# A 7x7 convolution of a 224x224 image on one core: the last tile's stage C loads spread over rounds, its inverse matrices built a tile earlier, a longer filler

## The chip, the cores and the metric

The kernel runs on one core of a Trainium2 chip. The metric is the device time of one execution in microseconds (us). Five engines take part: TensorE (PE in the profile, with PEld for its weight loads), VectorE (DVE), ScalarE (ACT), GpSimd (POOL) and SyncE (SP), which here only issues DMAs. Transfers run on 16 DMA engines.

## The reference, cut to what matters

```python
H = W = 224; C = 96; K = 7            # x: (1, H, W, C) bf16, w: (K, K, C, C) bf16
wp = jnp.pad(w, ((0, H - K), (0, W - K), (0, 0), (0, 0)))
Xf = rfft2(x.astype(f32), axes=(1, 2))
Wf = rfft2(wp.astype(f32), axes=(0, 1))
Yf = jnp.einsum('bhwi,hwio->bhwo', Xf, Wf)
y  = irfft2(Yf, s=(H, W), axes=(1, 2)).astype(bf16)
```

This is a circular convolution of the image with a 7x7 filter, with 96 channels in and 96 out. The output has the shape of the image.

## The kernel before, in words

The kernel does not use large Fourier transforms. Along the rows of the image (h) it works on 8 blocks of B = 28 rows, each lengthened by 6 rows to L = 34, and transforms these by a small real Fourier transform of 17 frequencies (NS = 17, numbered s). Along the columns (w) it convolves directly with the 7 taps, in a form that shares products between even and odd pixels. The columns are cut into NT = 7 tiles of 32 pixels; a tile is t, the last one is TL = 6.

There are three stages, and at any time they run for different tiles:

- Stage A (a_jobs, a_mm) loads rows of the image into xn and transforms them by matmuls with the matrix Fm; the results go to xf in SBUF.
- Stage B (b_round, one call for each frequency s) does the convolution for one frequency. It computes sums and differences J of xf on DVE (jit, called for three frequencies at a time), does 33 to 34 small matmuls with the transformed weights WF, and combines the two PSUM banks by an ACT operation (tt_), two DVE operations (u and v) and a last sum into yf, on POOL or, where DVE makes it, on DVE. put_y stores yf to a DRAM tile after every third frequency: scr for the earlier tiles, and for the last tile scra (frequencies 0 to 8) and three tiles scrb (9 to 11, 12 to 14, 15 and 16).
- Stage C (c_jobs, c_bank) turns the frequencies back into rows. For every tile but the last, load_t reads scr back in six groups (two halves h of the tile's columns, three groups gi of row blocks) into the buffers tt. A group takes 2 to 4 DMAs, 15 in all. Matmuls with the matrix G follow, evictions into yo, and DMAs of yo to the output (put_o). The last tile is done in another way, at the end of the program: scra is read into tl_a (two DMAs) and the scrb tiles into tl_b (load_b, three DMAs), and each of 16 PSUM banks gets a matmul of tl_a with the matrix GA (function first) and one of tl_b with a matrix GB (function second).

The order of work is written out by hand. The loop `for t in range(2, NT)` (line 792) runs stage B of tile t in rounds s = 0 to 16, with stage A of tile t + 1 and stage C of tile t - 1 filled in between by pace: a list of jobs, with first and last slot, where slots are counted as 2s and 2s + 1 and the fills of a round come after its first and after its second half. In the last tile one job of tile 4 and five of tile 5 are done in the rounds; the other five of tile 5 (half h = 1) stay for the end (`while cj`, line 838). Every engine runs its instructions in the order of the program, and this includes SP's DMA issues. The pools are: 8 PSUM banks, 6 buffers tt, 4 buffers yo, 4 buffers yf.

The parts that the change and the prediction touch:

- pump (line 676) issues the pending stage C loads while fewer than NTT = 6 groups are held; queue_c (line 681), called in round 3 of a tile, puts the six groups of tile t - 1 into the list and calls it. The end of each group's job also calls it (line 663). The variable late is always 0.
- g_parts (line 617) is a generator that builds GB and GA out of G. Its first 24 steps write GB, in tiles 3 and 4. The next one sets GA to zero on POOL and copies a first part; each further step copies one more by a DMA of SP. GA has four parts. It lies in the memory of Fm (line 783), which stage A of the last tile reads until round 12 of tile 5; the profile therefore calls it Fm.
- In tile 6, load_b(0) is issued in round SL[2] + 2 = 14, and the two DMAs into tl_a in round SA + 1 = 10. tl_a and tl_b lie in the memory of xf.
- From frequency 9 on, the last tile's puts are held in the list puts and issued by ACT (put(SE)): one after ACT's operation of round 12, the next at the end of round 16. The put of frequencies 15 and 16 is SP's.
- After the rounds, load_b(1) and load_b(2) are issued, the rest of stage C runs, then eight matmuls first, then WARM = 16 filler matmuls (line 857). The filler adds zeros to the eighth bank; it has no part in the result. Then come the 16 matmuls second with their evictions, by DVE and ACT in turn (tail_evac), the other eight first among them.

```python
    def queue_c(t):
        pend.extend((t, i % 3, i // 3) for i in range(6))
        pump()
```

Of the kernel before, what the change touches and what calls it, by code (L numbers as in the profile page):

```python
# [16 lines left out]
NS = L // 2  # L17
# [21 lines left out]
CQ = {2: (10, 2), 3: (8, 4), 4: (6, 7), 5: (3, 9), 6: (1, 5)}  # L39
NXN = 2  # L40
NP2 = 0
WARM = 16


def slot(s, part):
# [4 lines left out]
def kernel(  # L50
# [10 lines left out]
    TL = NT - 1  # L61
# [92 lines left out]
    SA = SL[1]  # L154
# [280 lines left out]
    def a_jobs(t):  # L435
        xf = new_xf(t)
        jobs = []
        for jg in range(2):
            if t == 0:
                jobs.extend(a_bank(t, xf, xh_bufs[jg], 0, 3, jg, 0))  # L440
            c = 2 * t + jg
            for h in range(2):
                for (q, n) in ((0, 3), (3, 3), (6, 2)):
                    jobs.extend(a_bank(t, xf, xn_bufs[c % NXN], h * PXC + 2 * q, n, jg, HALO + h * 8 + q))
            last = jobs.pop()

            def fin(last=last, c=c):
                last()
                if c + NXN < NCH:
                    load_x(c + NXN)  # L450
            jobs.append(fin)
        return jobs
# [4 lines left out]
    def jit(t, g):  # L457
        s0, s1 = JGB[g]
        n = s1 - s0
        xf = xf_tiles[t][0:C]  # L460
        xv = xf.rearrange("c p r s w j -> c p r s (w j)")
        b = jcount[0] % 3 if t < 2 else (jcount[0] - 2 * len(JGB)) % 2
        jcount[0] += 1
        Jb = J_bufs[b][0:C].rearrange("c (k s q) -> c k s q", k=7, s=3)
        for s in range(s0, s1):
            jbuf[(t, s)] = Jb[:, :, s - s0]

        def sub(o, i0, i1, op, cost):
            def f():
                load["v"] += 170 + cost * n / 1.92  # L470
                return VE.tensor_tensor(out=o, in0=i0, in1=i1, op=op)
            return f
        x0, x1 = xv[:, 0, :, s0:s1], xv[:, 1, :, s0:s1]
        pd, rd, sd, qd = x1.ap
        dpl = bass.AP(x1.tensor, x1.offset - NJ, [pd, [NJ, 2], rd, sd, qd])
        return [
            sub(Jb[:, 0:4, 0:n].rearrange("c (k r) s q -> c k r s q", r=2), dpl,
                x0.unsqueeze(1).to_broadcast([C, 2, 2, n, PP]), ALU.subtract, 4 * PP),
            sub(Jb[:, 4, 0:n], xv[:, 0, 0, s0:s1], xv[:, 0, 1, s0:s1], ALU.add, PP),
            sub(Jb[:, 5:7, 0:n], Jb[:, 0:4:2, 0:n], Jb[:, 1:4:2, 0:n], ALU.add, 2 * PP),  # L480
        ]
# [110 lines left out]
    def load_t(t, gi, h):  # L592
        j0, nj = CG[gi]
        n = nj * FR
        tt = t_pool.tile([128, TW // 2, 2 * C], BF16, name="tt")
        tt_tiles[(t, gi, h)] = tt
        sv = scr_tiles[t].rearrange("w j s (r e) -> (j s r) w e", r=2)
        n0 = n // 16 * 16
        w0, w1 = (h * 8, (h + 1) * 8) if gi < 2 else (h * 6, (h + 1) * 6)
        for (p0, p1) in ((0, n0), (n0, n)):  # L600
            dma(tt[p0:p1, 0:w1 - w0], sv[j0 * FR + p0:j0 * FR + p1, w0:w1])
        if gi == 2:
            for j, wa, wb, q0 in REST[h]:
                dma(tt[n:n + FR, q0:q0 + wb - wa], sv[j * FR:(j + 1) * FR, wa:wb])
# [6 lines left out]
    def load_b(i, eng, nh):  # L611
        sb = scr_tiles[(TL, 1 + i)].rearrange("w j s (r e) -> (j s r) w e", r=2)
        for h in range(nh):
            w0, w1 = h * TW // nh, (h + 1) * TW // nh
            dorder(eng.dma_start(out=tl_b[KO[i]:KO[i] + KB[i], w0:w1], in_=sb[:, w0:w1]))
# [12 lines left out]
    def c_bank(tt, yo, k, nj):  # L628
        pb = bank()
        TE.matmul(pb[0:nj * B, 0:4 * C], lhsT=G[0:nj * FR, 0:nj * B],  # L630
                  rhs=tt[0:nj * FR, 2 * k:2 * k + 2, :].rearrange("p w e -> p (w e)"), start=True, stop=True)
        evac(yo[0:nj * B, k * 4 * C:(k + 1) * 4 * C], pb[0:nj * B, 0:4 * C], 4 * C)

    def put_o(t, yo, p0, j, nj, wa, wb, q0):
        px = t * 2 * TW + 2 * wa
        dma(out[0, j * B:(j + nj) * B, px:px + 2 * (wb - wa), :].rearrange("h w c -> h (w c)"),
            yo[p0:p0 + nj * B, q0 * 2 * C:(q0 + wb - wa) * 2 * C])

    def c_jobs(t):
        jobs = []  # L640
        for h in range(2):
            for gi in range(3):
                j0, nj = CG[gi]
                hold = {}

                def mk_(ks, done, h=h, gi=gi, j0=j0, nj=nj, hold=hold):
                    def f():
                        if ks[0] == 0:
                            hold["yo"] = yo_pool.tile([4 * B, PXC * C], BF16, name="yo")
                        tt = tt_tiles[(t, gi, h)]  # L650
                        yo = hold["yo"]
                        for k in ks:
                            c_bank(tt, yo, k, 3 if gi < 2 or h == 0 or k == 0 else 2)
                        if not done:
                            return
                        if gi < 2:
                            put_o(t, yo, 0, j0, nj, 8 * h, 8 * h + 8, 0)
                        else:
                            put_o(t, yo, 0, j0, nj, 6 * h, 6 * h + 6, 0)
                            for j, wa, wb, q0 in REST[h]:  # L660
                                put_o(t, yo, nj * B, j, 1, wa, wb, q0)
                        held[0] -= 1
                        pump()
                    return f
                if gi < 2:
                    jobs.extend((mk_((0, 1), False), mk_((2, 3), True)))
                else:
                    jobs.append(mk_((0, 1, 2), True))
        return jobs

    NTT = 6
    held = [0]
    late = [0]
    pend = []

    def pump():
        while len(pend) > late[0] and held[0] < NTT:
            load_t(*pend.pop(0))
            held[0] += 1

    def queue_c(t):
        pend.extend((t, i % 3, i // 3) for i in range(6))
        pump()

    def warm(n):
        p = bank()
# [51 lines left out]
    def add(a, b, jobs):  # L738
        qs.append([a, b, jobs, len(jobs)])
# [19 lines left out]
    for r in range(NS + LAG):  # L759
# [4 lines left out]
        for t in range(2):  # L764
            s = r - LAG * t
# [25 lines left out]
    gp = g_parts()  # L791
    for t in range(2, NT):
        if t == TL:
            scr_tiles[t] = None
            scr_tiles[(t, 0)] = dr_pool.tile([TW, NJ, SA, 4 * C], BF16, name="scra")
            for i in range(len(KB)):
                scr_tiles[(t, 1 + i)] = dr_pool.tile([TW, NJ, KB[i] // (2 * NJ), 4 * C], BF16, name=f"scrb{i}")
        else:
            scr_tiles[t] = dr_pool.tile([TW, NJ, NS, 4 * C], BF16, name="scr")
        qs = []  # L800
        if t + 1 < NT:
            add(0, 26, a_jobs(t + 1))
        nold, nnew = CQ[t]
        k1 = 2 * NS if t < TL else 2 * NS - 9
        k0 = 12 if t == 2 else 3
        km = max(13, k0 + -(-(k1 - k0) * nold // (nold + nnew)))
        add(k0, km, cj[:nold])
        cn = c_jobs(t - 1)
        cj = cn[nnew:]
        add(km, k1, cn[:nnew])  # L810
        plan = {}
        for g, (s0, s1) in enumerate(JGB):
            if g + 1 < len(JGB) or t + 1 < NT:
                plan[s0 if g + 1 < len(JGB) else s0 - 1] = g
        for s in range(NS):
            now = ()
            if s in plan:
                g = plan[s]
                now = jit(t, g + 1) if g + 1 < len(JGB) else jit(t + 1, 0)
            if s == 3:  # L820
                queue_c(t - 1)
            if t in (3, 4) and s < 12 or t == TL and s < 4:
                next(gp, None)
            if t == TL and s == SL[2] + 2:
                load_b(0, DE, 1)
            if t == TL and s == 0:
                late[0] = 0
            if t == TL and s == SA + 1:
                sv = scr_tiles[(TL, 0)].rearrange("w j s (r e) -> (j s r) w e", r=2)
                for g in range(2):  # L830
                    dma(tl_a[g], sv[g * KA:(g + 1) * KA])
                late[0] = 0
                pump()
            b_round(t, s, fills(qs, 2 * s), fills(qs, 2 * s + 1), bool(now) if t < TL else s >= NS - 2 or (s < 12 and bool(now)), now)
    tail[0] = 2
    load_b(1, DE, 1)
# [19 lines left out]
    live = {k: first(*k) for k in order[:8]}  # L856
    for _ in range(WARM):
        TE.matmul(live[order[7]].rearrange("p (a b) -> p a b", a=12), lhsT=Fm.rearrange("p r s j -> p (r s j)")[:, 0:M4],
# [48 lines left out]
```

## Time and profile before

| | |
|---|---|
| median of 4 runs | 281.85 us (283.61, 284.4, 280.08, 280.1) |
| the profiled execution | 283.61 us, span 281.9 us |
| mean granted TensorE clock | 0.959 |
| busy, share of the span | PE 93%, PEld 85%, DVE 84%, ACT 66%, POOL 35% |
| chain that ended last | PE 66%, DVE 15%, DMA 8%, ACT 5% |
| tile 6 from about 235 us to the last round's end | 23.75 us (235.00 to 258.75) |
| from there to the first matmul of tl_b with GB | 13.61 us |
| from there to the end | 9.54 us |

The span runs from the first to the last instruction; the rest of the execution's time lies around it. A busy share is an average over stages with different limits, so a stage is read from its own window and from the waits that end last in it. In the timeline, times are us from the span's start; a row gives start, length, engine, line, operation and the names out<-in, and in brackets how long the engine was idle before it and what ended that. All operations are recorded with the line of one helper (L82), so they are told apart by the names. SPq and ACTq are rows of an engine's DMA issues.

### The profile page before, as it was taken

To read this page: it belongs to the slowest core of one execution; us is meant where nothing else is said; L and a number is where in the kernel's file an instruction comes from. 1 tells how busy PE (TensorE), PEld (TensorE's weight loads), DVE (VectorE), ACT (ScalarE), POOL (GpSimd) and SP (SyncE) were. 2 spreads that over 40 slices of the span, in tenths; PEclk is the share of its full clock that TensorE was granted. 3 is DMA by queue.
4 is the path that set the end of the run, shared out by engine and by line. 5 is a ranking of instruction groups with operands and counts; after the bars stand their busy time and mean duration, and the time that the engine had idled before them with its cause. 6 is when DMAs were issued, how large, how long until landed. Compare 5 with 4: busy or idle time off the path is not lost.

```text
span 281.9 us, 11544 instructions
## 1 busy us (share of the span) xinstructions
PE 262.9 (93%) x4810; PEld 239.8 (85%) x4810; DVE 237.6 (84%) x500; ACT 185.4 (66%) x459; POOL 99.1 (35%) x134
## 2 busy tenths in 40 slices
PE   8599999999979999999999999999999999799692
PEld 3299899999979999998989998899989998698371
DVE  6269999999997799999878899878988899989323
ACT  5079887665613986987888768887788854462222
POOL 2741023266455433422422242233243225345000
PEclk9959999999979999999999999999999999999668
DMA  8686243111211468988775875794868542867765
GB/s 164 110 227 163 63 131 109 44 44 45 86 45 44 155 188 181 274 251 238 229 194 142 262 216 186 171 274 146 255 168 201 192 160 69 192 177 170 203 179 183
DMA packets 45284, 46.01 MB, mean 163 GB/s; under 512 B 33746, under 2 KB 35974, under 8 KB 45136
## 3 DMA queue, kind: packets, MB, share of 16 engines
q1 hardware_dynamic: 44816, 43.78, 55.9%
q10 hardware_dynamic: 416, 1.49, 2.3%
q8 instruction: 38, 0.62, 1.0%
q14 instruction: 14, 0.11, 0.2%
HBM read 23.92 MB, written 21.33 MB: 161 GB/s over the span
## 4 chain that ended last, share of the span: by engine, by line
PE 66%; DVE 15%; DMA 8%; ACT 5%; SPq 2%; issue 2%; DVEq 0%; POOL 0%; ACTq 0%
PE pb L82 66%; DVE J L82 5%; DMA wq<-in_w_dram 4%; ACT xf L82 3%; DVE v L82 3%; DVE WF L82 3%; DMA out_dram<-yo 2%; DVE u L82 2%; ACT WF L82 2%; SPq L82 2%; DMA tt<-scr 1%; DVE xf L82 1%; DVE yf L82 1%; DVE tt L82 0%; DMA xn<-in_x_dram 0%
## 5 line engine op out<-in xcount | busy, mean ns | idle before, releaser
L82 PE MATMUL pb<-WF,J 96*128 96x96 bf16 x2898 | 166.8, 207 | 1.8 <-DVE J L82 0.6
L82 PEld LDWEIGHTS <-J 96*128 96x128 bf16 (+1 forms) x2910 | 144.1, 98 | 11.8 <-issue 4.4
L82 POOL TENSOR_TENSOR yf<-v,u 128x384 bf16<-128x384 f32 x87 | 87.0, 1016 | 143.0 <-issue 99.2
L82 ACT CAST xf<-pb 96x408 bf16<-96x408 f32 (+1 forms) x142 | 61.7, 484 | 4.8 <-PE pb L82 2.7
L82 PE MATMUL pb<-WF,xf 96*128 96x96 bf16 x952 | 60.6, 207 | 1.6 <-DVE WF L82 1.4
L82 DVE TENSOR_TENSOR J<-xf 96x1824 bf16<-96x1824 bf16 (+1 forms) x84 | 61.5, 770 | 0.1
L82 ACT CAST yo<-pb 84x384 bf16<-84x384 f32 (+1 forms) x122 | 52.0, 482 | 10.9 <-PE pb L82 5.8
L82 PEld LDWEIGHTS <-xf 96*128 96x128 bf16 x952 | 47.4, 98 | 1.9 <-issue 1.7
L82 PE MATMUL pb<-Fm,xn 118*128 118x136 bf16 x448 | 45.9, 222 | 0.2
L82 PE MATMUL pb<-tt,Gm 102*84 102x384 bf16 (+1 forms) x132 | 32.8, 331 | 5.3 <-DMA out_dram<-yo 3.0
L82 ACT CAST WF<-pb 96x480 bf16<-96x480 f32 (+1 forms) x58 | 30.0, 580 | 10.5 <-PE pb L82 10.5
L82 PEld LDWEIGHTS <-xn 118*128 118x128 bf16 x448 | 29.8, 98 | 1.0 <-issue 0.5
L82 PE MATMUL pb<-wq 98*128 98x120 bf16 (+1 forms) x288 | 24.6, 238 | 3.7 <-DMA xn<-in_x_dram 3.7
L82 PEld LDWEIGHTS <-wq 98*128 98x128 bf16 x288 | 21.7, 151 | 4.3 <-issue 4.2
L82 DVE TENSOR_TENSOR J<-J 96x912 bf16<-96x912 bf16 (+1 forms) x42 | 25.0, 594 | 0.0
L82 PEld LDWEIGHTS <-Gm 102*84 102x84 bf16 (+1 forms) x132 | 11.8, 117 | 7.1 <-DMA xf<-scra 3.3
L82 DVE TENSOR_TENSOR yf<-v,u 128x384 bf16<-128x384 f32 x24 | 16.2, 675 | 0.8
L82 DVE CAST xf<-pb 96x408 bf16<-96x408 f32 (+1 forms) x30 | 14.8, 532 | 0.6 <-PE pb L82 0.6
L82 DVE CAST WF<-pb 96x480 bf16<-96x480 f32 (+1 forms) x14 | 8.5, 612 | 6.2 <-PE pb L82 5.7
L82 PE MATMUL pb<-wu 128*128 128x512 bf16 x32 | 9.6, 476 | 1.1 <-DVE ct L82 1.1
L82 PEld LDWEIGHTS <-wu 128*128 128x128 bf16 (+1 forms) x40 | 4.7, 121 | 6.8 <-issue 3.3
L82 DVE CAST tt<-pb 112x384 bf16<-112x384 f32 x8 | 4.1, 554 | 7.3 <-PE pb L82 7.0
(393 smaller groups left out, 229.4 us busy)
## 6 DMA issues: line engine op xcount, KB each, us to landing
xn<-in_x_dram SPq DMA_DIRECT2D x13, 672.0 KB
scr<-yf SPq DMA_DIRECT2D x30, 288.0 KB
tt<-scr SPq DMA_DIRECT2D x24, 288.0 KB
out_dram<-yo SPq DMA_DIRECT2D x24, 252.0 KB
tt<-scr SPq DMA_DIRECT2D x12, 144.0 KB
out_dram<-yo SPq DMA_DIRECT2D x12, 126.0 KB
scr<-yf SPq DMA_DIRECT2D x6, 192.0 KB
scra<-yf SPq DMA_DIRECT2D x3, 288.0 KB
```

Of the source, the lines that this page charges most:

```text
L82: r = fn(*a, **k)
```

## The change

It has four edits.

1. The loads of stage C of tile 5, in tile 6: one group in round 3 and one more in each round from 4 on (pump takes a number of groups), and none at the end of a job (jlim is 0 in tile 6). In the other tiles the loads are issued as before. late goes.
2. The four steps of GA are taken in rounds 13 to 16 of tile 5 (NS - 4 and on) instead of rounds 0 to 3 of tile 6.
3. The two DMAs into tl_a are issued in round SA + 2 = 11 instead of 10.
4. WARM is 24 instead of 16.

```diff
-WARM = 16
+WARM = 24
...
                         held[0] -= 1
-                        pump()
+                        pump(jlim[0])
...
     NTT = 6
     held = [0]
-    late = [0]
+    jlim = [NTT]
     pend = []
 
-    def pump():
-        while len(pend) > late[0] and held[0] < NTT:
+    def pump(n=NTT):
+        while pend and held[0] < NTT and n:
             load_t(*pend.pop(0))
             held[0] += 1
-
-    def queue_c(t):
+            n -= 1
+
+    def queue_c(t, n=NTT):
         pend.extend((t, i % 3, i // 3) for i in range(6))
-        pump()
+        pump(n)
...
         if t == TL:
+            jlim[0] = 0
...
             if s == 3:
-                queue_c(t - 1)
-            if t in (3, 4) and s < 12 or t == TL and s < 4:
+                queue_c(t - 1, 1 if t == TL else NTT)
+            elif t == TL and s > 3:
+                pump(1)
+            if t in (3, 4) and s < 12 or t == TL - 1 and s >= NS - 4:
                 next(gp, None)
             if t == TL and s == SL[2] + 2:
                 load_b(0, DE, 1)
-            if t == TL and s == 0:
-                late[0] = 0
-            if t == TL and s == SA + 1:
+            if t == TL and s == SA + 2:
                 sv = scr_tiles[(TL, 0)].rearrange("w j s (r e) -> (j s r) w e", r=2)
                 for g in range(2):
                     dma(tl_a[g], sv[g * KA:(g + 1) * KA])
-                late[0] = 0
-                pump()
```

## The prediction

> **What bounds the kernel now.** I read the page first, by time slices: TensorE (PE) is full almost everywhere, so only places where it is not full, or where its clock is low, can give time.
>
> ```profile
> PE   8599999999979999999999999999999999799692
> PEclk9959999999979999999999999999999999999668
> ```
>
> PE dips in slice 34 (about 240 us) and slice 37 (about 261 us), and the granted clock is low in slices 38 and 39 and once in slice 12. The change touches only what follows 225 us. Next, the chain that ended last, from 239 us on (start, length, what):
>
> ```profile
> 239.36 3.42 DMA tt<-scr
> 242.92 13.51 PE pb L82 x283
> 256.43 6.66 DMA out_dram<-yo
> 263.09 12.72 PE pb L82 x47
> ```
>
> So the last tile waits twice for DMA: for the first loads of tile 5's stage C, and at the end of the last round. Third, the stages by windows (us, then busy time and count of PE, PEld, DVE, ACT, POOL, then granted clock, DMA share, GB/s); the windows are cut where the trace changes the clock, every 3.41 us:
>
> ```profile
> 77.95:81.36 3.41, 1.97 (x46) 1.85 (x44) 3.41 (x8) 0.41 (x1) 2.17 (x3) 1.00 0.09 30
> 81.36:84.77 3.41, 3.41 (x48) 3.41 (x45) 2.77 (x6) 0.49 (x2) 2.02 (x3) 0.50 0.17 64
> 238.37:241.79 3.42, 2.51 (x55) 2.22 (x51) 3.42 (x9) 0.82 (x2) 0.56 (x1) 1.00 0.72 200
> 258.85:262.27 3.42, 1.20 (x9) 0.73 (x7) 3.28 (x9) 0.00 (x0) 0.00 (x0) 1.00 1.02 182
> 265.68:269.09 3.41, 3.41 (x12) 2.36 (x11) 0.28 (x1) 0.00 (x0) 0.00 (x0) 0.50 0.50 139
> 269.09:272.51 3.42, 3.42 (x12) 2.32 (x11) 0.00 (x0) 0.00 (x0) 0.00 (x0) 0.50 0.88 250
> ```
>
> A window with PE busy for 1.97 or 1.20 us is followed by half clock, one with 2.51 us is not. Fourth, the timeline of SyncE's DMA queue (SPq):
>
> ```profile
> 234.93 1.65 SPq L82 DMA_DIRECT2D Fm<-Gm  x2
> ...
> 238.94 10.02 SPq L82 DMA_DIRECT2D tt<-scr  x15
> 249.01 0.80 SPq L82 DMA_DIRECT2D Fm<-Gm  x1
> 249.92 1.13 SPq L82 DMA_DIRECT2D scra<-yf  x1
> ...
> 251.60 0.35 SPq L82 DMA_DIRECT2D scra<-yf  x1
> 254.97 1.36 SPq L82 DMA_DIRECT2D xf<-scra  x2
> 256.43 5.54 SPq L82 DMA_DIRECT2D out_dram<-yo  x4
> ```
>
> The 15 stage C loads hold the queue for 10 us; the scra stores of rounds 5 and 8 stand behind them, and the two reads of scra behind those. Last, the tail in the timeline of all engines:
>
> ```profile
> 258.75 1.30 PE L82 MATMUL pb<-tt,Gm 102*84 102x384 bf16 x7
> ...
> 262.11 0.33 ACTq L82 DMA_DIRECT2D scrb<-yf  x1
> 262.56 1.61 ACT L82 CAST yo<-pb 84x384 bf16<-84x384 f32 x4 [3.74 <-DMA xf<-scra]
> 263.08 1.63 PE L82 MATMUL pb<-tt,Gm 102*84 102x384 bf16 x4 [3.03 <-DMA out_dram<-yo]
> ...
> 267.24 5.33 PE L82 MATMUL pb<-xn,Fm 118*112 118x384 bf16 x16
> ...
> 272.36 0.89 PE L82 MATMUL pb<-xf,GB 128*112 128x384 bf16 x4
> ```
>
> ScalarE's store of scrb (ACTq) is stuck until the first read of scra has landed, and four evictions stand behind it; PE, out of banks, idles 3.03 us. The reason lies in the records of the DMAs: each takes the next of eight completion semaphores in program order, and so first waits for the DMA eight before it. Eight before this store is the first xf<-scra. After the stall the clock is halved from 262.27 to 272.51, so the 16 filler matmuls take 0.32 us each instead of the 0.163 us that matmuls of the same 384 columns take from 273 us on. The final matmuls follow the filler at once. The DMA packets show the last tl_b read over at about 270.4: here the filler, not DMA, ends last, by 1.9 us.
>
> **The change part by part.** The sum is against the profiled execution, 283.61 us (span 281.9 and 1.7 around it).
>
> *The GA build to tile 5.* One memset (0.19 us on POOL) and four Fm<-Gm DMAs leave tile 6; three stand ahead of the loads: 0.84 + 0.76 + 0.74 = 2.3 us of SP. Only part is on the path, as the scra store of round 2, next in the queue, needs POOL's sum, over at 238.08 (start 236.12 and 1.96). It was issued at 238.43, so it and the first load come 0.35 us earlier, and PE's wait for that load (1.43 us at 242.92) shrinks by as much: **-0.35**. DVE is full in 238.37:241.79 but has gaps after 246, so the gain survives. In tile 5 the four DMAs stand ahead of output stores and the scr stores of rounds 14 and 16; SP waits there anyway (3.4 us for POOL before 234.49). The memset waits for the last stage A matmuls of round 12, and POOL sat idle 3.15 us before 231.52: cost 0, and 0.8 us for one DMA if a store stood behind it in time.
>
> *Loads by rounds.* Nothing is added: 15 DMAs as before. SP runs its queue in order and is not tied to rounds, so the first three groups (8 DMAs) still go in one burst. But the scra store of round 5 now stands behind 8 loads, not 15 and a Fm DMA, and the others behind it. The store of round 8 is then bound by its own sum on POOL (246.32 and 2.12 = 248.44), not by the queue: about 248.6 to 249.0 instead of 251.60. From there to the reads of scra took 3.4 us (254.97): they go at about 252. The second half's loads go out at 243.5 to 248 and are first used at 258.4.
>
> *scra reads one round later (about 1.4 us).* In the queue they only fall behind one output store (0.35 us), evicted by 250.3; the landing of the store still decides. Cost 0; 0.35 if not. But it changes the count: eight before ScalarE's last scrb store there is now that output store, issued at about 250.4, not a scra read. So the ACT wait of 3.3 us (258.81 to 262.11) goes, and the fifth yo buffer, whose output store took 3.99 us to issue at 256.43 and held up DVE till 264.9, is free as well.
>
> *Tail.* What is late next: VectorE. Its last round's work ends at 260.61 - 0.35 = 260.26, then six evictions at 0.47 us spacing (four in 1.94 us) end at about 263.1; ScalarE's five end before. The fifth of the eight "first" matmuls followed VectorE's last eviction before (265.96) and will again: 263.1 + 4 x 0.163 = 263.75 for the start of the filler, against 267.24: **-3.5** (the 0.35 within it).
>
> *Filler 16 to 24.* At full clock 24 x 0.163 = 3.9 us, against 5.12: **-1.2**, of which the eight added ones cost 1.3. At half clock they would cost 2.6. So the final matmuls start at 267.65 instead of 272.36: -4.7, and the 9.5 us behind them stay: 283.6 - 4.7 = 278.9. Does DMA allow it? The last scrb store goes at about 260.3 instead of 264.21; from there to the last read's end took 6.2 us: 266.5, so there is 1.1 us to spare.
>
> *The clock.* In a window like 258.85:262.27 I count 12 matmuls of 384 columns, 1.95 us, between the rows 1.97 (dropped, with smaller gaps) and 2.51 (not). By columns streamed it is 0.56 of full against 0.49 and 0.59, nearer to the one that stayed. I take no drop, and keep the other end: +3.0 us, if PE runs at half clock from 262.3 until a window full of filler ends at 269.1.
>
> The Trainium skill, "TensorE: Matmul & The Clock Gate" (Part 1), says that half rate follows an idle window of about 3.4 us and that gaps under some 3 us are safe. The row of 77.95 speaks against it: the clock fell with PE busy more than half of the window. By the rule nothing drops and the time is the 278.9 above; by the row it may be 281.9. The same page's advice to keep PE busy speaks for a long filler; the windows here show it costs 0.163 us each once the clock is up.
>
> The early half-clock window at 81.36 costs at most half of 3.41 = 1.7 us and is not touched; of the four runs shown (283.61, 284.4, 280.08, 280.1, median 281.85) the profiled one is 1.8 above the median. With that window I get 278.9, without it 277.2; I forecast the middle, **278.0 us**, 1.4% under the median.
>
> **The rivals.**
> 1. *The clock drops in the tail all the same.* For: 1.95 is not far from 1.97, and the windows lie where they like. Price +1.7 (one window at half clock) to +3.0: 279.7 to 281.0.
> 2. *DMA takes the filler's place.* If SP's last scrb store goes more than 1.1 us later than 260.3, its reads end last; a 3.99 us issue like that at 256.43 would do it. At before's place, 264.21, the gain is 1.9 (no clock loss): 281.7 or, without the early window, 280.0.
> 3. *Slower: the stall stays and the filler is longer.* If ScalarE's store still waits till about 262 (its eighth-before DMA, or a sum on POOL, is late), the clock falls as before and eight more matmuls come at the end: 1.3 us (after 272.5) to 2.6 (half clock) over the median: 283.1 to 284.4. It decides once that store is issued after 262.1. Against it: the count of DMAs above, and POOL's sums ending at 258.60.
> 4. *More than forecast.* VectorE's evictions or the wait at 242.92 shrink more (up to 1.43): below 276.
>
> **How the numbers follow.** Forecast 0.55 (own range 276.0 to 279.5), rival 1 0.22, rival 2 0.10, rival 3 0.08, rival 4 0.05. The range 276.0 to 282.0 takes in the first three and leaves out the last two. Two per cent, about what a measurement of this kernel can tell from no change, is 5.6 us: under 276.2 lie rival 4 and a little of the forecast, 0.10; above 287.5 lies only a rival 3 worse than priced, 0.06; within, 0.84.
>
> **What would show it.** Right: the scra store of round 8 near 249 and its reads near 252; ScalarE's last scrb store near 258.5 to 259; no PE gap over 1 us between 258 and 264; filler at 0.163 us; final matmuls near 267.6. Wrong: a DMA named in ScalarE's wait in the last round; filler at 0.32; an idle gap between the filler and the final matmuls (rival 2); SP held up in tile 5, or PE waiting for tt beyond round 6.

## The result, and the profile after

The changed kernel takes 280.41 us (median of 49 runs, 276.17 to 284.79); the kernel before, beside it, 282.12 us (75 runs). The ratio on record is 0.9885, with a 95% interval of 0.9862 to 0.9908: faster by about 1.2%. It leaves out executions that took over 1.5% longer than the fastest of the same kernel, about half of the changed kernel's and fewer of the other's; the medians contain them, and by them the ratio is 0.9939.

Two profiled executions of the changed kernel are read here, since they differ in the clock. The first took 283.64 us (span 281.9, mean granted clock 0.961), the second 278.81 us (span 277.0, clock 0.976; it is the run r2_changed below). These are the page's time slices of PE and of its granted clock in the first:

```profile
PE   8399999999979999999999999999999999799992
PEclk9959999999989999999999999999999999779988
```

and the clock's row in the second:

```profile
PEclk9979999999977999999999999999999999999997
```

The dip of PE near 261 us that before's row had (a 6) is gone in the first row. In its clock row the two sevens, from about 240 to 254 us, and the eight from about 268 us are lower than what the second execution has there; the windows below place them. First the tail of the second execution, in the timeline of all engines (start, length, engine, line, operation, out<-in, count, and in brackets the idle time before and its releaser):

```profile
258.31 0.33 ACTq L82 DMA_DIRECT2D scrb<-yf  x1
258.41 1.75 PE L82 MATMUL pb<-tt,Gm 102*84 102x384 bf16 x9
...
260.20 2.86 DVE L82 CAST yo<-pb 84x384 bf16<-84x384 f32 x6
...
260.80 0.95 PE L82 MATMUL pb<-xf,Fm 72*112 72x384 bf16 x4
...
262.03 1.40 PE L82 MATMUL pb<-xf,Fm 72*112 72x384 bf16 x4 [0.28 <-DMA xf<-scra]
...
263.27 4.06 PE L82 MATMUL pb<-xn,Fm 118*112 118x384 bf16 x24
...
267.58 0.67 PE L82 MATMUL pb<-xf,GB 128*112 128x384 bf16 x3 [0.24 <-DMA xf<-scrb]
```

ScalarE's last store of scrb goes at the round's end and waits for nothing. The nine matmuls of the rest of stage C run in one piece, where before they came as 7 and 4 with 3.03 us of idle time between. VectorE's six evictions set the start of the filler (the last is over at 263.06, and the last of the eight "first" matmuls, the rows with pb<-xf,Fm, starts at 263.11), and 24 filler matmuls take 4.06 us in place of 16 in 5.33. But the bracket of the last line is new: the final matmuls now wait 0.24 us for the read of tl_b. The chain that ended last, of the same execution, says so too:

```profile
242.57 17.15 PE pb L82 x348
259.73 0.57 DVE yf L82
260.29 0.02 issue
260.31 4.42 DMA scrb<-yf
264.73 0.02 issue
264.74 2.71 DMA xf<-scrb
267.45 0.14 issue
267.58 3.88 PE pb L82 x22
```

Between the last round and the final matmuls the chain now runs through the store of the last frequencies (4.42 us until its data can be read) and their read (2.71 us), not through the filler.

By stages, against the profiled execution of before: the time from the last round's end to the first matmul of tl_b fell from 13.61 to 9.17 us (-4.44), and the time from the last scr store of tile 5 (round 16) to the last round's end from 24.26 to 23.80 us (-0.46); together -4.90. After the first matmul of tl_b, 9.42 us follow (9.54 before).

The same tail in the first execution:

```profile
262.15 0.33 ACTq L82 DMA_DIRECT2D scrb<-yf  x1
262.24 1.75 PE L82 MATMUL pb<-tt,Gm 102*84 102x384 bf16 x9
262.77 1.61 ACT L82 CAST yo<-pb 84x384 bf16<-84x384 f32 x4 [0.46 <-DMA out_dram<-yo]
...
264.04 2.87 DVE L82 CAST yo<-pb 84x384 bf16<-84x384 f32 x6
...
267.23 5.51 PE L82 MATMUL pb<-xn,Fm 118*112 118x384 bf16 x24
...
272.58 0.81 PE L82 MATMUL pb<-xf,GB 128*112 128x384 bf16 x4
```

It has the same order and no stall either, and all of it lies 3.8 us later, with a filler of 5.51 us. The windows of that execution (start:end, length, busy time and count of PE, PEld, DVE, ACT and POOL, then granted clock, DMA share, GB/s) show why:

```profile
239.44:242.85 3.41, 2.10 (x45) 1.80 (x42) 3.41 (x9) 0.80 (x2) 0.97 (x2) 1.00 1.00 236
242.85:246.27 3.42, 2.78 (x29) 2.52 (x30) 3.23 (x5) 1.19 (x3) 0.98 (x2) 0.50 0.83 173
246.27:249.68 3.41, 3.41 (x40) 3.12 (x38) 0.91 (x2) 1.33 (x4) 1.00 (x1) 0.50 0.81 201
263.33:266.75 3.42, 2.95 (x13) 1.28 (x12) 3.31 (x8) 1.53 (x4) 0.00 (x0) 1.00 0.89 217
266.75:270.16 3.41, 3.27 (x12) 2.17 (x11) 0.16 (x1) 0.00 (x0) 0.00 (x0) 0.50 0.67 188
```

The clock is halved twice: for two windows after PE's wait for the first loads in tile 6 (45 matmuls, busy 2.10 us), and for one window in the tail. The first makes the stretch from the last scr store to the last round's end 27.10 us long in place of 23.80; the second makes the tail 10.34 us in place of 9.17.

In the second execution the two windows at the same places are these:

```profile
240.02:243.44 3.42, 2.45 (x48) 2.22 (x49) 3.39 (x8) 0.91 (x3) 1.95 (x2) 1.00 1.11 227
260.50:263.92 3.42, 2.91 (x14) 1.51 (x13) 2.56 (x6) 0.52 (x2) 0.00 (x0) 1.00 0.91 254
```

48 and 14 matmuls in place of 45 and 13, and the clock stayed up. In both places the kernel is close to the point where the clock falls. In tile 6 PE's wait for the loads differs too (1.34 us in the first execution, 0.97 in the second), so it is not shown how much of the difference comes from where the windows lie.

### The profile page after: what moved, and what is told of

Its sections match the earlier page's. It is cut to its first block, busy times and chain, and to the rows that moved or that the text cites. A ratio compares the mean times of both kernels' runs of the same rounds, so it can differ in the third digit from the quotient of the medians.

```text
span 281.9 us, 11563 instructions
## 1 busy us (share of the span) xinstructions
PE 264.4 (94%) x4818; PEld 242.3 (86%) x4818; DVE 238.1 (84%) x500; ACT 185.6 (66%) x459; POOL 99.0 (35%) x134
## 4 chain that ended last, share of the span: by engine, by line
PE 66%; DVE 18%; DMA 7%; ACT 4%; issue 2%; POOL 1%; SPq 0%; POOLq 0%; DVEq 0%; ACTq 0%
PE pb L82 66%; DVE J L82 5%; DMA wq<-in_w_dram 4%; DVE v L82 4%; ACT xf L82 3%; DVE WF L82 3%; DVE u L82 2%; DMA tt<-scr 1%; DVE yf L82 1%; DVE xf L82 1%; DVE yo L82 1%; POOL yf L82 1%; ACT WF L82 1%; DMA scrb<-yf 1%; SPq L82 0%
## 5 line engine op out<-in xcount | busy, mean ns | idle before, releaser
L82 PE MATMUL pb<-WF,J 96*128 96x96 bf16 x2898 | 168.5, 208 | 1.7 <-DVE J L82 0.8
L82 PEld LDWEIGHTS <-J 96*128 96x128 bf16 (+1 forms) x2910 | 145.7, 99 | 12.0 <-issue 4.4
L82 PE MATMUL pb<-WF,xf 96*128 96x96 bf16 x952 | 61.6, 208 | 1.7 <-DVE WF L82 1.4
L82 PEld LDWEIGHTS <-xf 96*128 96x128 bf16 x952 | 48.3, 99 | 2.2 <-issue 1.8
L82 DVE TENSOR_TENSOR WF<-WF 96x1440 bf16<-96x1440 bf16 x10 | 10.1, 1013 | 0.0
```

The lines of the kernel that those rows point to most:

```text
L82: r = fn(*a, **k)
```

## The experiments

The theory was that of the prediction: ScalarE's last store of scrb was held by a read of scra eight DMAs before it, the edits together take this wait away, and the tail then gains some 4.4 us. The rivals were that one edit alone does it, that the longer filler costs what it adds, and that the clock decides. All filler matmuls add zeros to a bank and have no part in the result; no run leaves out anything else. "Tail" is the time from the last round's end to the first matmul of tl_b, "final part" from there to the end of the span, both from the profile of the run. The column of medians is the median of all executions by that of the kernel before beside them.

| run | edits | ratio to before (95%) | medians | tail, us | final part, us |
|---|---|---|---|---|---|
| before | none | 1 | 1 | 13.61 | 9.54 |
| changed, first and second | all four | 0.9885 (0.9862 to 0.9908), 0.9913 (0.9868 to 0.9959) | 0.9939, 0.9912 | 10.34, 9.17 | 9.32, 9.42 |
| p1_filler | filler alone | none | 1.0065 | 10.39 | 9.57 |
| p2_loads | loads by rounds alone | 0.9956 (0.9922 to 0.9991) | 0.9938 | 10.19 | 9.77 |
| p3_reads | reads in round 11 alone | 0.9985 (0.9931 to 1.0039) | 1.0018 | 10.14 | 10.38 |
| p4_ga | GA in tile 5 alone | 0.9962 (0.9925 to 1.0000) | 0.9982 | 11.75 | 9.32 |
| q1_filler16 | all but the filler | 0.9963 (0.9928 to 0.9998) | 0.9928 | 9.12 | 9.34 |
| q2_reads10 | all but the reads' round | 1.0022 (0.9985 to 1.0060) | 0.9961 | 13.56 | 9.43 |
| q3_first2, r3_first2 | changed, first group in round 2 | 0.9892 (0.9839 to 0.9945), 0.9888 (0.9837 to 0.9938) | 0.9888, 0.9879 | 10.46, 10.44 | 9.40, 9.69 |
| q4_first2_filler16 | the same with 16 fillers | 0.9948 (0.9909 to 0.9987) | 0.9922 | 10.79 | 11.10 |
| r1_reads_filler | reads' round and filler | 0.9944 (0.9904 to 0.9984) | 0.9984 | 11.19 | 9.36 |
| r4_first2_spread | q3 with fillers between | 0.9881 (0.9842 to 0.9920) | 0.9888 | 9.89 | 9.37 |

A profile is one execution, so a tail can hold a clock drop that the ratio doesn't weigh in the same way; the ratio says what an edit is worth, the profile how. Where the ratio and the medians differ, the size of an effect is less sure than its interval says.

### Each edit alone, on the kernel before

```diff
# p1_filler
-WARM = 16
+WARM = 24
# p2_loads: edit 1 of the change alone (pump, queue_c, jlim)
-                queue_c(t - 1)
+                queue_c(t - 1, 1 if t == TL else NTT)
+            elif t == TL and s > 3:
+                pump(1)
# p3_reads
-            if t == TL and s == SA + 1:
+            if t == TL and s == SA + 2:
# p4_ga
-            if t in (3, 4) and s < 12 or t == TL and s < 4:
+            if t in (3, 4) and s < 12 or t == TL - 1 and s >= NS - 4:
```

> Before with the filler of 24 alone. My theory: the stall of PE at the end of the last round stays at about 3 us, the filler already ends after the last tl_b read, so eight more matmuls come on top: 1.3 us (full clock) to 2.6 us (half), ratio to before 1.004 to 1.009. Rival, that the filler is what gains (it brings the clock back before the final matmuls): ratio under 1, by up to 1.7 us, 0.994.

> Before with the loads by rounds alone; the reads of scra stay in round 10, ahead of an output store. My theory, that ScalarE's last scrb store waits for the DMA eight before it, still a read of scra here: the reads go out some 3 us earlier against the end of the last round, so that the wait shrinks from 3.7 us to under 1 us, but the output store behind the reads is late and holds up a yo buffer; ratio 0.988 to 0.995. Rival, that only the earlier flow of DMAs counts: as the whole change or better, 0.985 or less, since the filler is short.

> Before with the reads of scra in round 11 alone: they go out as late as before (some 3.8 us before the end of the last round), but eight DMAs before ScalarE's store there is now an output store that went out earlier. My theory: ScalarE's wait for a read of scra is gone, PE's stall at the end of the last round is under 1 us, ratio 0.988 to 0.995. Rival, that the time of the reads decides: PE waits about 3 us as before, ratio 1.00.

> Before with the GA build in tile 5 alone. My theory: the first load of the last tile goes out 0.35 us earlier, and nothing else changes: ratio 0.998 to 1.000. Rival, that the four DMAs hold up SP in tile 5 or ahead of the 15 loads more than that: 0.99 or 1.005.

*The filler alone* came out at 283.5 us (median of 6 runs, 278.25 to 288.04; before 281.68), too scattered for a ratio: the cost that I expected is neither shown nor ruled out, and there is no sign of a gain. Its profile holds a clock drop of 6.8 us in tile 6, from 242.5 us on, and with it something that had not been expected. From the timeline of its tail:

```profile
261.74 1.75 PE L82 MATMUL pb<-tt,Gm 102*84 102x384 bf16 x9
262.27 1.61 ACT L82 CAST yo<-pb 84x384 bf16<-84x384 f32 x4 [0.46 <-PE pb L82]
```

The stall is not there, though the reads of scra are in round 10 as before. Tile 6 is slower by the drop, DMA is not, so the reads go out 8.0 us ahead of the last round's end and have landed in time. This execution, which lost time to the clock in tile 6, had no stall to lose.

*The loads by rounds alone* gained 0.44%, a little less than expected. In its profile the first read of scra, out 4.97 us ahead of the round's end, landed 5.0 us later, and the store goes 0.08 us after that: a wait of some 0.2 us is left of it. What is late instead is ScalarE's last eviction, behind an output store:

```profile
264.11 0.47 ACT L82 CAST yo<-pb 56x384 bf16<-56x384 f32 x1 [1.89 <-DMA out_dram<-yo]
```

*The reads in round 11 alone*: no measurable gain (0.9985, where 0.988 to 0.995 had been expected), although its profile has the stall gone. The stall is gone by the order alone: ScalarE's store went at 257.58, and the first read of scra landed only at 258.90. From the timeline of PE:

```profile
257.68 1.75 PE L82 MATMUL pb<-tt,Gm 102*84 102x384 bf16 x9
...
262.56 2.76 PE L82 MATMUL pb<-xn,Fm 118*112 118x384 bf16 x16
...
267.82 1.11 PE L82 MATMUL pb<-xf,GB 128*112 128x384 bf16 x4 [2.49 <-DMA xf<-scrb]
```

and its windows:

```profile
264.80:268.21 3.41, 0.92 (x7) 0.49 (x6) 0.00 (x0) 0.01 (x1) 0.00 (x0) 1.00 0.84 248
268.21:271.62 3.41, 3.41 (x13) 2.23 (x12) 2.09 (x4) 1.86 (x4) 0.00 (x0) 0.50 0.57 167
```

The nine matmuls run in one piece. Then 16 fillers at full clock are over at 265.3, PE is idle for 2.49 us, and the window in which it idles halves the clock for the next: the final part takes 10.38 us in place of some 9.4. With the stall away, the old filler is too short.

*GA in tile 5 alone*: 0.9962. From the last scr store of tile 5 to the first load of tt it took 4.07 us in place of 4.46, 0.39 less (0.35 had been worked out), and 4.07 again in both executions of the changed kernel. The stall stays:

```profile
259.87 1.61 ACT L82 CAST yo<-pb 84x384 bf16<-84x384 f32 x4 [3.08 <-DMA xf<-scra]
260.40 1.63 PE L82 MATMUL pb<-tt,Gm 102*84 102x384 bf16 x4 [2.37 <-ACT yo L82]
```

It is shorter by 0.66 us both on ACT (3.74 before) and on PE (3.03), so a part of this edit's gain is in the tail: the store of round 8 goes 7.66 us ahead of the round's end in place of 7.15, and the reads 4.21 in place of 3.78, without the loads by rounds. In tile 5 the four DMAs and the memset held nothing up that a profile shows: PE has no wait over 0.3 us there, in before or here.

So the three edits with a ratio bring 0 to 0.4% each, and none of them alone brings the 1.2%.

### One edit taken back, from the changed kernel

```diff
# q1_filler16
-WARM = 24
+WARM = 16
# q2_reads10
-            if t == TL and s == SA + 2:
+            if t == TL and s == SA + 1:
# q3_first2, the same as r3_first2 (not a step back: one step on)
-            if s == 3:
+            if s == (2 if t == TL else 3):
# q4_first2_filler16: q3_first2 and
-WARM = 24
+WARM = 16
```

> The changed kernel with the filler of 16 as before. My theory: in the profile of the changed kernel the last tl_b read ends 7.4 us after the last round, while the filler of 24 ends 10.2 us after it (8.7 at full clock), so a filler of 16 gives back 1.1 to 1.3 us: the final matmuls start 7.5 to 9.1 us after the last round, time 0.9955 of the changed kernel's. Rival, that the longer filler pays by keeping the clock up for the 16 final matmuls and their evictions: equal or slower than the changed kernel, ratio to before 0.988 to 0.995.

> The changed kernel with the reads of scra in round 10 again, ahead of an output store. My theory (the output store then goes out some 4 us late behind the reads and holds a yo buffer of the last evictions, as it did with the loads by rounds alone: 1.4 us of PE idle 4.4 us after the last round): ACT waits 1 to 2 us for an output store in the tail, PE idles over 1 us there; the final matmuls start at least as late, about 10 us after the last round; time 0 to 1 us over the changed kernel. Rival, that the move of the reads does nothing once the loads are spread: no such wait.

> The changed kernel with the first of the six groups issued in round 2 instead of 3, ahead of the scra store of round 2. My theory, that what the change left over in the last tile is PE's wait of 1.3 to 1.5 us for this load, and the clock drop that follows it in executions whose window falls on it: the load goes out 1.4 us earlier, the wait is under 0.3 us, the clock stays at 1.0 around 240 us; ratio to before 0.980 to 0.985. Rival, that VectorE sets the pace there (it is busy without a gap): PE waits for VectorE instead, no gain over the changed kernel, 0.988.

> The two together, first group in round 2 and filler of 16. By my theory the gains add: 0.975 to 0.981 of before. By the rivals: 0.988 to 0.995.

*The reads back in round 10* undo the whole gain by the ratio, 1.0022 of the time before; by the medians, 0.9961, they leave a part of it. The timeline:

```profile
251.94 1.18 SPq L82 DMA_DIRECT2D xf<-scra  x2
...
259.16 0.33 ACTq L82 DMA_DIRECT2D scrb<-yf  x1
...
259.61 1.61 ACT L82 CAST yo<-pb 84x384 bf16<-84x384 f32 x4 [3.63 <-DMA xf<-scra]
260.13 1.63 PE L82 MATMUL pb<-tt,Gm 102*84 102x384 bf16 x4 [2.92 <-ACT yo L82]
```

I had expected that the earlier loads would leave at most 1 us of it, with a wait for an output store. In fact the stall is back in full (3.63 us on ACT, 2.92 on PE). The store of round 8 was issued 9.10 us ahead of the round's end (7.15 in before), but the reads only 3.97 us ahead of it (3.78 in before), and the first of them landed 7.1 us after its issue.

The DMA records of the traces show the count at work. In all fourteen profiles of this study ScalarE's last store uses the same completion semaphore, and the DMA that had it before is the first read of scra in the five with the reads in round 10, an output store in the nine with round 11. In the three that stall (before, p4_ga, q2_reads10) the store goes 0.08 us after that read has landed: 262.03 and 262.11, 259.35 and 259.43, 259.08 and 259.16. In p1_filler and p2_loads the read had landed earlier, or just then. In none of the nine is the store held up, and in three of them (p3_reads, r1_reads_filler and the second execution of the changed kernel) it goes before the first read has landed. (In r1_reads_filler the bracket of ACT's evictions names a read of scra, but with the 0.46 us that the others have too.) So a read that is early enough does as well, but another DMA eight places ahead does it whatever the time of the read.

The same count holds SyncE's last store of scrb. In before it stands eight places behind the second read of scra and went 0.06 us after that had landed (264.15), 5.46 us after the round's end. In the second execution of the changed kernel it stands behind the first read, which had landed at 259.24, and went at 260.31, as soon as VectorE's last sum was made, 1.90 us after the round's end.

*The filler back to 16* gives 0.9963 against 0.9885 and 0.9913: by the ratios the longer filler is worth some 0.5 to 0.8%, but the second interval overlaps, and by the medians (0.9928 against 0.9939 and 0.9912) there is no difference. I had expected 16 to be better by 0.0045; the ratios speak for the rival, that the long filler pays. The profile of this run doesn't show the reason, as its 16 fillers were stretched to 4.31 us by half clock and covered the wait. The pair with the first group in round 2 does. q4_first2_filler16 (0.9948, against 0.9892 and 0.9888 with 24, by the medians 0.9922 against 0.9888 and 0.9879; 0.975 to 0.981 by my theory, which missed), from the timeline of PE:

```profile
263.89 2.76 PE L82 MATMUL pb<-xn,Fm 118*112 118x384 bf16 x16
...
269.80 1.40 PE L82 MATMUL pb<-xf,GB 128*112 128x384 bf16 x4 [3.15 <-DMA xf<-scrb]
```

and its windows:

```profile
266.50:269.91 3.41, 0.27 (x2) 0.14 (x2) 0.00 (x0) 0.00 (x0) 0.00 (x0) 1.00 0.67 188
269.91:273.32 3.41, 3.41 (x12) 2.31 (x12) 1.67 (x3) 1.92 (x4) 0.00 (x0) 0.50 0.68 190
```

This is the picture of p3_reads again: 3.15 us idle, half clock, and a final part of 11.1 us in place of 9.4. So how the filler pays is shown; how much it pays over all executions is less sure.

*The first group in round 2* takes away PE's wait for tt in tile 6: it is gone from the list of PE's waits, where DVE's J and u come next at 0.6 and 0.5 us. The expected ratio of 0.980 to 0.985 was missed (0.9892, and 0.9888 in r3_first2); what is won in tile 6 (23.34 us from the last scr store of tile 5 to the round's end, against 23.80) comes back in the tail, 10.46 and 10.44 us: SyncE's last store of scrb goes 2.35 and 3.50 us after the round's end, against 1.90. Why it is later is not shown. Against the changed kernel the difference lies within the intervals.

### What the pair is worth, and one step further

```diff
# r1_reads_filler, from the kernel before
-WARM = 16
+WARM = 24
-            if t == TL and s == SA + 1:
+            if t == TL and s == SA + 2:
# r2_changed: the changed kernel as it is
# r4_first2_spread: q3_first2 and two fillers after each of the first seven "first" matmuls
-    live = {k: first(*k) for k in order[:8]}
+    live = {}
+    for k in order[:8]:
+        live[k] = first(*k)
+        for _ in range(2 if k != order[7] else 0):
+            TE.matmul(live[order[0]], lhsT=Fm, rhs=xn, start=False, stop=False)
```

(The operands of the last line are cut down here to their names; it adds zeros to the first bank.)

> Before with two edits, the reads of scra in round 11 and the filler of 24; the loads in one burst and the GA build in tile 6 as before. My theory now, that the order of these reads takes ScalarE's wait away and the filler spans the time until tl_b lands: no PE idle over 1 us after the last round, the 16 final matmuls at full clock, 9.3 to 9.5 us from the first of them to the end; ratio 0.988 to 0.993, most of the change's gain. Rival, that the loads by rounds are needed: 0.995 to 1.00.

> The changed kernel itself, to stand beside the others of this call on the same chip: ratio to before 0.986 to 0.991; about half of its runs within 277 to 280 us and half above 280, if a clock drop in the last tile at about 243 us comes in some of them only.

> The changed kernel with the first group in round 2, again, beside the changed kernel. My theory: without PE's wait in the last tile no window there falls under the limit, so that the runs above 280 us are rare; median 1.5 to 2.5 us under that of the changed kernel. Rival, that it only shifts the wait: the same share of runs above 280, median within 0.5 us.

> The one before with 14 more filler matmuls, two after each of the first seven matmuls named first, where PE waits for VectorE's evictions (they add zeros to the first bank). My theory, that the sparse stretch 1.3 to 4.7 us after the last round drops the clock for one window and costs the filler 1.7 us: no drop there, final matmuls 8.5 to 9.0 us after the last round instead of 10.3, or as soon as tl_b has landed; time 0.5 to 1.5 us under the kernel with the first group in round 2. Rival, that DMA sets the end anyway: PE idles before the final matmuls, no gain.

*Reads and filler without the other two edits* reach 0.9944; 0.988 to 0.993 had been expected. The reads go out only 3.78 us before the last round's end, and the "first" matmuls wait for them (0.71 and 0.96 us), with a clock drop behind. SyncE's last store of scrb now waits for the first of them (landed at 262.64, store at 262.70). That the loads by rounds and GA carry the rest is likely by this; the intervals of this run and of the changed kernel beside it overlap.

*The changed kernel again* gives 0.9913. Of its 12 executions 4 took over 280 us, where about half had been expected.

*The first group in round 2 once more* (0.9888): none of its 6 executions took over 280 us, as my theory said, but the median is only 0.9 us under the changed kernel's, where 1.5 to 2.5 had been expected. Its profile still ends on DMA, with the 24 fillers run out:

```profile
267.31 0.83 PE L82 MATMUL pb<-xf,GB 128*112 128x384 bf16 x4 [1.51 <-DMA xf<-scrb]
```

*With 14 more fillers between the "first" matmuls*, PE has no idle time ahead of the final matmuls and no clock drop in tile 6 or the tail:

```profile
261.13 4.06 PE L82 MATMUL pb<-xn,Fm 118*112 118x384 bf16 x24
265.03 0.82 PE L82 MATMUL pb<-xf,GB 128*112 128x384 bf16 x4
```

This execution, 276.22 us, is the shortest of any profiled here, but the ratio, 0.9881 (0.9842 to 0.9920), is not to be told from the changed kernel's, and the median (278.20 us) is no better than that of r3_first2 (277.95), where a gain of 0.5 to 1.5 us had been expected. The tail is 9.89 us where 8.5 to 9.0 had been expected: the last read of tl_b had landed at 264.55, so now the fillers end last.

## Why the prediction was right, and where it was off

- **The stall: right, and for the reason given.** ScalarE's store no longer waits for a read of scra, PE's 3.03 us of idle time are gone, VectorE's six evictions (2.86 us) set the start of the filler. Taking back the reads' round alone brings all of it back (q2_reads10). SyncE's last store of scrb, which the forecast moved from 264.21 to 260.3 without saying what had held it, went at 260.31; in before the same count had held it.
- **The tail: -4.44 us in the second execution, where -3.5 and -1.2, less the 0.35 counted in tile 6, make -4.35.** GA: -0.39 at the first load and -0.46 to the round's end, where -0.35 was forecast. The sum against one execution held: -4.90 measured, -4.7 forecast. That it fits so closely is in part luck, as two errors cancel. The filler started at 263.27, not 263.75, since one "first" matmul follows VectorE's last eviction and not four; in before the fifth merely started as that eviction ended, one of a row that ran at half clock every 0.32 us. And from the start of the filler to the final matmuls it took 4.31 us, not 3.9, since DMA ended last.
- **The median: 278.0 forecast, 280.41 measured; the ratio 0.9863 forecast (278.0 by 281.85), 0.9885 measured.** The time lies in the range 276.0 to 282.0, but not in the forecast's own 276.0 to 279.5: it lies where rival 1 was priced (279.7 to 281.0). So the median came right by the width of the range, and the sum by one of two profiles (beside the other runs, the median of the changed kernel was 278.87). The forecast ratio is near the edge of the measured interval. What was off is the step from the profiled execution to the median: a gain of 3.85 us on the median was forecast, as if most executions had what the profile showed (4.9 us as measured). By the two ratios the gain is 0.87 to 1.15% of 282 us, 2.5 to 3.2 us, half to two thirds of the 4.9; by the medians it is 1.7 and 2.5 us. What a profile shows of the rest: where the clock falls in tile 6 (the first execution, p1_filler and q1_filler16), 3.3 us are lost there, and in the one such profile of a kernel with the old reads (p1_filler) there is no stall for the change to remove; in the first execution too the first read had landed (260.22) well before ScalarE's store (262.15), so that the order had nothing to remove. In all executions of the changed kernel on record the time goes with the mean granted clock: 0.985 to 0.992 in those under 278 us, 0.961 in five of the eight over 283 us. In which stage the clock fell is known only where there is a profile, so the share of tile 6 in the 1.7 to 2.4 us between the two is open.
- **The clock in the tail: no drop was taken; rival 1 is in one of the two profiles.** 13 matmuls in 263.33:266.75 were followed by half clock, 14 in 260.50:263.92 were not. The price was +1.17 us on the tail (10.34 against 9.17), less than the +1.7 to +3.0 given. A drop in tile 6 was not priced at all; it costs 3.3 us.
- **The filler: probably a wrong sign, and a DMA term that was too short.** "Of which the eight added ones cost 1.3" holds only while the filler ends last. DMA was given 1.1 us to spare: 6.2 us from the last store of scrb to the end of the last read, from 260.3. That counts to the read's last packet (270.45); its last completion signal came at 271.07, 6.86 us after the store. In the second execution the store did go at 260.31, the last signal came 7.14 us later, and the final matmuls waited 0.24 us for it. So rival 2 was at the door at 24 fillers, and with 16 it is inside in p3_reads and q4_first2_filler16: 2.5 to 3.2 us idle, and a final part, at half clock, that is 1.0 to 1.7 us longer. By the ratios the eight fillers are worth 0.5 to 0.8% where a cost of 0.5% had been worked out; by the medians, 0.3 to 0.4% or nothing.
- **The reads of scra: about 252 forecast, 253.80 measured.** The store of round 8 went at 249.61 (forecast 248.6 to 249.0), but from there to its reads it took 4.2 us, not 3.4. It cost no wait of ScalarE's store, which here was decided by order and not by time.
- **Edits that don't add.** The forecast summed terms. The runs give 0.44, 0.15 and 0.38% for three edits alone, which is 0.97% together and not far from the whole. But taken away from the whole, the reads' order costs 1.1 to 1.4% by the ratios (q2_reads10), and the filler 0.5 to 0.8%. The profiles show how the edits depend on each other: the order removes a wait, the filler covers the next one, and the earlier loads make room for both.

The Trainium skill ("TensorE: Matmul & The Clock Gate", Part 1) names an idle window as what brings the clock down. The rows above disagree: after 263.33:266.75 it fell with PE busy 2.95 of 3.42 us.

## What to carry to other kernels

When a store waits at its issue for a DMA that has nothing to do with it, count the DMAs of the program between the two: moving a transfer by one place in the order took away a stall that the edits meant to issue it earlier had left in place (q2_reads10 against the changed kernel: 3.63 us of ACT's time, ratios 1.0022 against 0.9885). A removed wait uncovers the next, so look at what ends second; a filler that bridges to it is worth its length if the idle time would halve the clock of what follows. And price an edit against more than one profiled execution: here a clock drop in another stage changes what there is to gain.

## What the runs showed of the hardware

- The recorded busy time of PE does not tell whether the clock falls. These are single windows, of q3_first2 and then of r4_first2_spread:

```profile
258.06:261.47 3.41, 2.80 (x12) 1.24 (x11) 3.26 (x7) 1.20 (x3) 0.00 (x0) 1.00 0.79 200
261.47:264.89 3.42, 3.42 (x12) 2.32 (x12) 0.00 (x0) 0.00 (x0) 0.00 (x0) 0.50 0.70 169
```

```profile
256.98:260.39 3.41, 3.32 (x20) 2.43 (x20) 2.81 (x7) 0.77 (x2) 0.00 (x0) 1.00 0.77 202
```

  With 12 matmuls, busy for 2.80 us, the clock fell; before, it stayed with 2.51 us busy (238.37:241.79, 55 matmuls). A matmul of 384 columns is recorded 0.33 us long, but in a row one starts every 0.163 us, so a few long matmuls look busier than they are. An estimate, from the columns that stream inside each window of 3.41 us by the recorded ends of the matmuls and the granted clock (the fullest window has some 8100): the clock fell after every window with under 3300 and after none with over 4700; between these both occur. Some records can be missing, so no sharp limit is shown.
- It came back after one to three windows at half clock. In before's 265.68:269.09 PE was busy throughout, and the next window was still at half clock; in the first execution of the changed kernel 266.75:270.16, with PE busy for 3.27 us, was followed by full clock. What decides is not shown.
- From the issue of a store to the issue of the reads that wait for it (scra of round 8) it took 2.52 us (251.23 to 253.75 in p1_filler) to 5.13 us (246.81 to 251.94 in q2_reads10).
- A read's last completion signal came 0.6 us after its last packet: 270.45 and 271.07 in before, 266.82 and 267.45 in the second execution of the changed kernel, where the matmul that waited for it started at 267.58.
